# A band mask that is loaded, and one that GpSimd builds: block-sparse attention with a feed-forward layer on one core

## The chip, the cores and the metric

One Trainium2 chip, one core of it. The metric is the device time of one execution in microseconds (us). The kernel before takes 613.03 us, the median of 3 runs (612.43 to 613.39). The engines are TensorE (PE, with its weight loads as PEld), VectorE (DVE), ScalarE (ACT), GpSimd (POOL), and SyncE (SP), whose queue issues every DMA named here.

## The reference

Attention in 4 batches of 8 heads, 768 positions of 64 dimensions. Each query sees the keys at a distance under 16 and, beside them, one summary key and value for each of the 24 blocks of 32 keys: the maximum of the block's keys and the mean of its values.

```python
k_sum = k.reshape(B, H, nb, 32, D).max(axis=3)
v_sum = v.reshape(B, H, nb, 32, D).mean(axis=3)
scores_l = where(|i - j| < 16, scale * q @ k.T, -1e9)
scores_s = scale * q @ k_sum.T + log(32)
a = softmax(concat([scores_l, scores_s]))
x = a @ concat([v, v_sum])
h = x @ w_in;  g = maximum(0.01 * h, h);  out = g @ w_out
```

The result x is 3072 rows of 512; w_in is 512 by 2048, w_out 2048 by 512. All of it is float32.

## The kernel before

The rows are cut into eight chunks of 384 rows (c = 0 to 7, two a batch). Attention of a chunk is 12 units: four pairs of heads (p = 0 to 3) by three tiles of 128 queries. A unit goes through these steps, with the names of its tiles: scores (`s`, PE, line 371), sum with the mask and row minimum of the negated score (`e` and `m`, DVE, line 376), exponential with row sum (`e` and `z`, ACT, line 383), division (DVE, lines 420 to 428), transposition (`t`, PE, line 388), copy (`pt`, ACT, line 439), product with the values (`o`, PE, line 394), and a high part and a low part of x (ACT line 445, DVE line 448). The feed-forward layer of a chunk (PE, `h` line 724, `a` lines 743 to 745) takes each product three times, by high and low parts. The weights come in pieces of 512 KB, and DVE and ACT split each into two parts (lines 680 to 693); the pieces stream in during the first two chunks. Later chunks get their attention beside feed-forward work of earlier ones.

What a pair of heads needs in chunk 0: keys `kn` (410 KB; DVE takes the block maxima, line 248, and copies them into place, line 331, and ACT copies the key windows, line 315), queries `q` (197 KB), value windows `v` (295 KB), and for all pairs together the block means of v. Those are made for batch 0 by six matmuls (`vps`, line 284) from three pieces `vb` (524 KB each) with a matrix of 1/32; ACT copies the result (line 289), and GpSimd copies it behind each pair's value windows (line 327). In the program, `L327` waits for the load of `v` and for the means.

`mask` is one tile of 128 partitions by 404 float32: three versions of the mask of 120 columns (24 for the block scores, which hold sqrt(64) * log 32, and 96 for the window, 0 or -8e9; the first, an inner and the last tile of queries), and behind them 44 columns with the matrix for the block means (called `share` in the change). Line 230 loads it from HBM, where the host had laid it out.

The order of the work is written by a planner in the program (`Plan`, lines 71 to 155). Each operation has a cost, a priority and what it depends on, and the planner replays them: an engine that is free takes the ready operation of lowest priority. The instructions of each engine then stand in that order, and each engine works them off in it. For loads the planner counts 250 bytes a ns, one after the other. `LOADS` fixes the order of the first loads on SP's queue; where one of them must wait (for a buffer), all behind it wait. Two queries' buffers alternate (`KR = 2`), three of values (`VR = 3`), six of `big` for keys, `vb` and weight pieces; the exponentials `e` and the copies `pt` have two buffers of two units each (`ER`, `PTR`).

Where the planner foresees that PE has nothing to do before the feed-forward layer begins, the program puts matmuls on zeros in its queue (`spare`, line 1343), as many as fill the foreseen gap less 300 ns. PE executes them whether or not it could go on earlier.

The constants `PLACE`, `PL`, `VT`, `KP`, `KS`, `XW`, `W0` and `OFF` are offsets of priorities: `OFF` holds those of the steps of a unit in chunks 0 and 1, `VT` that of the block means, `KP` and `KS` those of the key maxima of batch 0, `PL` that of the later steps of pairs of units, `W0` that of the first weight piece. `USQ` is used nowhere.

Of the kernel before, what the change touches and what calls it, by code (L numbers as in the profile page):

```python
# [13 lines left out]
ALU = mybir.AluOpType  # L14
AX = mybir.AxisListType

B, H, S, D = 4, 8, 768, 64
NP = H // 2
BLK, WIN = 32, 16
NS = S // BLK  # L20
# [3 lines left out]
LK = 120  # L24
# [17 lines left out]
P2 = 56.037475  # L42
XB = (0, 1, 1, 0)
SB = 2
PLACE = {0: (0.0, 1.0), 1: (13.07, 0.61), 2: (24.128751, 0.979249), 3: (33.570341, 0.464868), 4: (39.468202, 0.605071), 5: (53.449962, 0.361478), 6: (58.988368, 0.872963), 7: (67.160878, 1.199752)}
PLACE.update({c: (59.84 + UPC * (c - 6), 1.0) for c in range(8, NCH)})
LATE = 23.650498
RS = 8
# [2 lines left out]
AHEAD = 2.529455  # L51
BACC = {"dynamic_dma_scratch_size": 1024}

PL = -1.175
WS = 0.721
WS2 = 0.376
LD = 3.541
XP = 2.116
VT = -1.915
KP = -1.757  # L60
KS = -4
XW = 1
B1 = 2.589473
B2 = 2.761653
USQ = 1.589009
WT = 1.15
W0 = -1.523
WO = 1.029
CUT = 1
WIDE = 12  # L70
OFF = {('rec', 0): (-2.762, -0.036), ('ex', 0): (3.066, -0.083), ('pt', 0): (0.079, -0.747), ('tr', 0): (-2.274, -0.362), ('ttr', 0): (-5.883, 0.424), ('nrm', 0): (0.274, -0.908), ('qk', 0): (-7.35, 0.368), ('xlo', 0): (1.352, 0.149), ('xhi', 0): (-1.785, 0.164), ('av', 0): (-2.699, -0.545), ('pt', 1): (3.776, 0.667), ('xlo', 1): (2.15, -1.485), ('tr', 1): (-0.4, -0.633), ('ttr', 1): (5.204, 0.013), ('qk', 1): (5.855, -0.039), ('av', 1): (-6.304, -0.442), ('ex', 1): (1.869, -0.057), ('nrm', 1): (1.368, -0.059), ('rec', 1): (3.066, -0.235), ('xhi', 1): (-5.461, -0.101)}
LOADS = [('kn', 0, 0), ('q', 0, 1), ('q', 0, 0), ('kn', 0, 1), ('mask',), ('vb', 0, 0), ('kn', 0, 2), ('vb', 0, 2), ('q', 0, 2), ('vb', 0, 1), ('kn', 0, 3), ('w', 0, 0), ('v', 0, 0), ('v', 0, 1), ('q', 0, 3), ('v', 0, 2), ('v', 0, 3), ('w', 1, 0), ('w', 0, 1), ('w', 1, 1)]


class Plan:
# [84 lines left out]
def ACT(n, psum=False, extra=0):  # L160
    return (51 if psum else 93) + 0.833 * n + 93 * extra
# [6 lines left out]
def POOL(n):  # L168
    return 130 + 1.0 * n


def build(tc, ctx, a):
    nc = tc.nc
# [11 lines left out]
    mask = cst.tile([128, 3 * LK + 44], F32, name="mask")  # L185
# [23 lines left out]
    P = Plan()  # L209
# [3 lines left out]
    def load_op(name, prio, fn, **kw):  # L213
        first[name] = P.op("SP", 550, prio, fn, **kw)
        return first[name]

    def new(tag, key, shape, dt=F32, bufs=2, src=None):
        tl[key] = (src or st).tile(shape, dt, tag=tag, name="_".join(str(x) for x in key), bufs=bufs)
        return tl[key]

    def bigs(key):
        n = int(P.slot[key][3:])
        tl[key] = big[:, 1024 * n:1024 * n + 1024]
        return tl[key]
# [2 lines left out]
        tag = tag or P.slot[key]  # L227
        return new(tag, key, [128, 512], src={"h": ps_h, "a": ps_acc, "s": ps_s, "t": ps_t}[tag[0]], bufs=1)

    mask_op = load_op(("mask",), -8.7, lambda: nc.sync.dma_start(out=mask, in_=a["mask"]), size=128 * (3 * LK + 44) * 4)  # L230

    LEAD = UPC + LD
    ksum_op, vsum_op, k_op, v_op, x_op, w_op = {}, {}, {}, {}, {}, {}
# [41 lines left out]
    def v_mean_pe(t):  # L275
        def load(j):
            x = bigs(("vb", 0, j))
            nc.sync.dma_start(out=x.rearrange("p (t d) -> p t d", t=2), in_=a["v0"][j])

        def mm(j, i):  # L280
            if i + j == 0:
                new("a1", ("vps",), [128, 512], src=ps_acc, bufs=1)
            n = 2 * j + i
            nc.tensor.matmul(tl["vps",][:NS], mask[:, 3 * LK + 20 - 4 * n:3 * LK + 44 - 4 * n], tl["vb", 0, j][:, 512 * i:512 * i + 512],  # L284
                             start=n == 0, stop=n == 5)

        def copy():
            tl["vsum", 0] = new("out", ("vs0",), [128, 512], bufs=TPC)[:NS]
            nc.scalar.copy(tl["vsum", 0], tl["vps",][:NS])
        prev = [mask_op]  # L290
        for j in range(3):
            o = load_op(("vb", 0, j), t - 4.5 + 0.1 * j, lambda j=j: load(j), alloc=[("big", ("vb", 0, j), 0)], size=128 * 4096)
            for i in range(2):
                prev = [P.op("PE", 856, t, lambda i=i, j=j: mm(j, i), after=[o] + prev, use=[("vb", 0, j), ("vps",)],
                             alloc=[("a1", ("vps",), 1)] if i + j == 0 else [])]
        vsum_op[0] = P.op("ACT", ACT(512, True), t + 0.1, copy, after=prev, use=[("vps",)], alloc=[("out", ("vsum", 0), TPC)])


    def operands(c, p, t, ahead):
# [12 lines left out]
        def windows(j):  # L312
            k = tl[kk][:, T:].rearrange("p (t r k) -> p t r k", r=2, k=LK)[:, :, j, NS:LK]
            x = tl[kw][:, 64 * j:64 * j + T].rearrange("p (t r) -> p t r", r=128)[:, :, 0:96]
            nc.scalar.copy(k, x)  # L315
# [18 lines left out]
        if cb:  # L334
            kn_op[kw] = load_op(kw, t - 1.3 - ahead, load_k, alloc=[("big", kw, 0)], size=128 * (T + 2 * WIN) * 4)
        ks = [P.op("ACT", ACT(TPC * 96), t - 0.6 + (0 if b else XW), lambda j=j: windows(j), after=[lq, kn_op[kw]], use=[kk, kw]) for j in range(2)]
        lv = load_op(("v", c, p), t - 0.6 - ahead, load_v, alloc=[("v", kv, VR)], size=96 * TPC * 1024)
        if c:
            ls = load_op(("s", c, p), t - 0.3, load_s, after=[lv, vsum_op[b]], use=[kv, ("vsum", b)], size=2 * NS * TPC * 512)
        else:  # L340
            ls = P.op("POOL", POOL(2 * TPC * 128), t - 0.3, load_s, after=[lv, vsum_op[b]], use=[kv, ("vsum", b)])
        ks.append(P.op("DVE", DVE(2 * TPC * NS, True), t - 0.5 + (0 if b else KS), k_s, after=[lq, ksum_op[b, p]], use=[kk, ("ksum", b, p)]))
        k_op[c, p], v_op[c, p] = ks, [lv, ls]

    def place(u, at=None):
        c = min(u // UPC, NCH - 1) if at is None else at
        t, d = PLACE.get(c, (UPC * c, 1.0))
        return t + d * (u - UPC * c)
# [52 lines left out]
    def unit(u):  # L401
        c, r, p, i, mv = where(u)
        K = lambda n: (n, u)
        v, m = place(u), u // 2
        off = lambda n: OFF[n, c][0] + OFF[n, c][1] * r if (n, c) in OFF else 0.0
        kk, kv = ("k", c, p), ("v", c, p)
# [92 lines left out]
    def pair(m):  # L499
# [4 lines left out]
        gs, gt, go = [("g", m + n, ph) for n in range(3)]  # L504
        v1, v2 = v + 2 + PL, v + 4 + PL
        kk, kv = [("k", c, x) for x in sorted({p, p1})], [("v", c, x) for x in sorted({p, p1})]
# [755 lines left out]
    for c in range(NCH):  # L1262
        b, cb = divmod(c, CPB)
        for p in range(NP):
            t = place(TPC * (c * NP + p))
            if cb == 0:
                if b:
                    v_mean(b, p, place(TPC * c * NP) + (B1 if b == 1 else B2) - TPC - 0.5 + 0.6 * p, 0)
                elif p == 0:
                    v_mean_pe(VT)  # L1270
                k_max(b, p, t - TPC - 0.3 + (B1 if b == 1 else B2 if b else KP), 0 if b else 9 - 3 * p)
        for p in range(NP):
            t = place(TPC * (c * NP + p))
            operands(c, p, t, 0 if c else 7 - 2.5 * p)
    for f in range(NF):
        for w in range(2):
            weights(f, w, LEAD - WT + min(f, SPL) * WS + max(f - SPL, 0) * WS2 + WO * w + (W0 if f == 0 else 0))
    for u in range(UPC):
# [42 lines left out]
    for n in range(6):  # L1321
        f = (1, 5, 11)[n % 3]
# [5 lines left out]

    for x, y in zip(LOADS, LOADS[1:]):
        first[y]["behind"] = first[x]  # L1330
# [18 lines left out]
def layouts(q, k, v, moe_w_in, moe_w_out):  # L1349
    import numpy as np  # L1350

    f = np.float32
    qa = q.reshape(B, NP, 2, CPB, T, D).transpose(0, 3, 1, 2, 5, 4).reshape(B, CPB, NP, 128, T)
    kp = np.zeros((B, NP, 128, S + 2 * WIN), f)
    kp[..., WIN:WIN + S] = k.reshape(B, NP, 2, S, D).transpose(0, 1, 2, 4, 3).reshape(B, NP, 128, S)
    vpad = np.zeros((B, NP, S + 2 * WIN, 128), f)
    vpad[:, :, WIN:WIN + S] = v.reshape(B, NP, 2, S, D).transpose(0, 1, 3, 2, 4).reshape(B, NP, S, 128)
    va = np.zeros((B, CPB, NP, 96, 2 * TPC, 128), f)
    for c in range(CPB):
        for i in range(2 * TPC):  # L1360
            o = c * T + 64 * i
            va[:, c, :, :, i] = vpad[:, :, o:o + 96]
    vb = np.ascontiguousarray(v.reshape(B, NP, 2, NS, BLK, D).transpose(0, 1, 3, 2, 5, 4)).reshape(B, NP * NS, 128, BLK)
    v0 = np.ascontiguousarray(v[0].transpose(1, 0, 2).reshape(3, 2, 128, H * D).transpose(0, 2, 1, 3))
    wi = moe_w_in.reshape(4, 128, NF, 128).transpose(2, 1, 0, 3).reshape(NF, 128, 512)
    w = np.ascontiguousarray(np.stack([wi, moe_w_out.reshape(NF, 128, DM)], axis=1)).view(np.int64)
    mk = np.full((128, 3, LK), -8.0e9, f)
    for vnt, t0 in enumerate((0, 128, S - 128)):
        for r in range(128):
            for w_ in range(96):  # L1370
                key = t0 - WIN + w_ + r // 64 * 64
                if 0 <= key < S and abs(t0 + r - key) < WIN:
                    mk[r, vnt, NS + w_] = 0.0
    mk[:, :, 0:NS] = math.sqrt(D) * math.log(BLK)
    mean = np.zeros((128, 44), f)
    mean[np.arange(128), 20 + np.arange(128) // BLK] = 1.0 / BLK
    mk = np.ascontiguousarray(np.concatenate([mk.reshape(128, 3 * LK), mean], axis=1))
    return {"q": np.ascontiguousarray(qa), "k": kp, "v": va, "v0": v0, "vb": vb, "w": w, "mask": mk}


# [16 lines left out]
```

## Time and profile before

| | |
|---|---|
| median of 3 runs | 613.03 us |
| the profiled execution | 612.7 us |
| its span (first to last instruction) | 610.9 us |
| PE busy in the span | 604.9 us (99%) |
| DVE, ACT, POOL busy | 469.7, 351.1, 4.4 us |
| spare matmuls (line 1343) | 164 |
| mean granted PE clock | 1.0 of full speed |
| DMA over the span | 130 MB, 213 GB/s |

The span is 1.8 us shorter than the execution's time. "Busy" of PE holds the spare matmuls too: the real work of PE is less. In the rows below, a line such as L376 is a line of the kernel before; out<-in are names of tiles; PEclk is the granted clock of PE as a share of full speed; a DMA share near 1 means that all 16 DMA engines were at work.

### The profile page before, as it was taken

The numbers are of one execution on the slowest core, as the hardware profiler recorded it, in microseconds if no ns is written. First come the engines' busy times: TensorE is split into PE (matmuls) and PEld (weight loads), VectorE is DVE, ScalarE is ACT, GpSimd is POOL, SyncE is SP. The second block draws the span as 40 slices with busy tenths as digits, with TensorE's granted clock in tenths as the row PEclk, the third lists the DMA queues.
The fourth block names the chain that finished last, engine by engine and source line by source line (L and its number), as shares of the span: only waits on it lengthen the run. The fifth ranks groups of instructions, "written<-read, shape, count | busy, mean of one in ns | idle before, by whom it ended". The sixth has DMA issues, their size and how long they took to land.

```text
span 610.9 us, 12895 instructions
## 1 busy us (share of the span) xinstructions
PE 604.9 (99%) x4676; PEld 540.1 (88%) x4676; DVE 469.7 (77%) x1281; ACT 351.1 (57%) x965; POOL 4.4 (1%) x10
## 2 busy tenths in 40 slices
PE   9999999999999999999999999999999999999997
PEld 6688889889888889999898897989889899999996
DVE  5899999953989995536688875877987783868687
ACT  5899996553776676416466665753717262606060
POOL 0200000000000000000000000000000000000000
PEclk9999999999999999999999999999999999999999
DMA  8898998896878826526497563866757484757552
GB/s 298 245 282 273 288 301 245 269 325 198 288 240 244 252 64 197 167 65 190 120 292 229 175 219 120 280 202 216 257 183 231 143 236 143 237 152 229 156 155 103
DMA packets 82926, 129.99 MB, mean 213 GB/s; under 512 B 7024, under 2 KB 50608, under 8 KB 82864
## 3 DMA queue, kind: packets, MB, share of 16 engines
q1 hardware_dynamic: 82864, 129.18, 68.1%
q8 instruction: 37, 0.61, 0.4%
q14 instruction: 25, 0.20, 0.1%
HBM read 97.72 MB, written 29.36 MB: 208 GB/s over the span
## 4 chain that ended last, share of the span: by engine, by line
PE 91%; DVE 4%; ACT 2%; DMA 1%; issue 0%; SPq 0%; DVEq 0%
PE L L1229 19%; PE h L724 12%; PE X L1090 8%; PE W L1090 8%; PE Z L1090 7%; PE B_a L1040 5%; PE a L744 4%; PE a L745 4%; PE a L743 4%; PE Y L1090 4%; PE B_s L1040 2%; PE B_to L1040 1%; ACT e L383 1%; PE vps L284 1%; DMA big<-in_k_dram 1%; DVE big L687 1%
## 5 line engine op out<-in xcount | busy, mean ns | idle before, releaser
L724 PE MATMUL h<-x,win_hi 128*128 128x384 f32 x320 | 82.7, 339 | 0.0
L383 ACT ACTIVATE e<-e,m 128x120 f32<-128x120 f32 x192 | 73.7, 388 | 3.7 <-DVE m L376 3.5
L1229 PE MATMUL L<-wout_hi,win_hi 128*128 128x512 f32 x168 | 66.5, 396 | 0.0
L1229 PE MATMUL L<-wout_hi,win_lo 128*128 128x512 f32 x168 | 65.7, 391 | 0.0
L1229 PE MATMUL L<-wout_lo,win_hi 128*128 128x512 f32 x168 | 65.6, 391 | 0.0
L724 PEld LDWEIGHTS h<-x,win_hi 128*128 128x128 f32 x320 | 57.6, 188 | 2.3 <-issue 0.2
L724 PE MATMUL h<-x,win_lo 128*128 128x384 f32 x160 | 53.8, 336 | 0.0
L743 PE MATMUL a<-wout_hi,ghi 128*128 128x512 f32 x120 | 48.4, 403 | 0.0
L745 PE MATMUL a<-wout_hi,glo 128*128 128x512 f32 x120 | 47.3, 394 | 0.0
L744 PE MATMUL a<-wout_lo,ghi 128*128 128x512 f32 x120 | 47.1, 392 | 0.1
L1229 PEld LDWEIGHTS L<-wout_hi,win_lo 128*128 128x128 f32 x168 | 31.5, 188 | 6.8
L383 ACT ACTIVATION_READ_ACCUMULATOR e<-e,m 128x1 f32 x192 | 36.7, 191 | 0.0
L1229 PEld LDWEIGHTS L<-wout_lo,win_hi 128*128 128x128 f32 x168 | 31.6, 188 | 5.7
L1229 PEld LDWEIGHTS L<-wout_hi,win_hi 128*128 128x128 f32 x168 | 31.6, 188 | 5.7
L734 DVE TENSOR_TENSOR glo<-gs,ghi 128x384 fp32r<-128x384 f32 x40 | 22.1, 554 | 17.0 <-ACT gs L728 16.3
L731 ACT ACTIVATE ghi<-h 128x384 fp32r<-128x384 f32 x40 | 19.6, 490 | 25.9 <-PE h L724 25.9
L1186 ACT COPY P<-X 128x384 f32<-128x384 f32 x19 | 9.0, 473 | 37.0 <-PE X L1090 36.9
L724 PEld LDWEIGHTS h<-x,win_lo 128*128 128x128 f32 x160 | 30.0, 188 | 0.0
L745 PEld LDWEIGHTS a<-wout_hi,glo 128*128 128x128 f32 x120 | 22.5, 188 | 5.4 <-DVE glo L734 0.4
L315 ACT COPY k<-big 128x288 f32<-128x288 f32 x64 | 24.8, 434 | 4.1 <-DMA big<-in_k_dram 4.0
L744 PEld LDWEIGHTS a<-wout_lo,ghi 128*128 128x128 f32 x120 | 22.6, 188 | 3.9 <-DVE wout_lo L693 0.4
L743 PEld LDWEIGHTS a<-wout_hi,ghi 128*128 128x128 f32 x120 | 22.6, 188 | 3.3
(620 smaller groups left out, 1625.9 us busy)
## 6 DMA issues: line engine op xcount, KB each, us to landing
win_hi<-sums SPq DMA_DIRECT2D x73, 256.0 KB
win_lo<-sums SPq DMA_DIRECT2D x71, 256.0 KB
big<-in_w_dram SPq DMA_DIRECT2D x32, 512.0 KB
sums<-big SPq DMA_DIRECT2D x32, 512.0 KB
v<-in_v_dram SPq DMA_DIRECT2D x32, 288.0 KB
big<-in_k_dram SPq DMA_DIRECT2D x16, 400.0 KB
k<-in_q_dram SPq DMA_DIRECT2D x32, 192.0 KB
wout_hi<-sums SPq DMA_DIRECT2D x21, 256.0 KB
```

The source lines that it names most:

```text
L315: nc.scalar.copy(k, x)
L383: nc.scalar.activation(out=e[:, n], in_=e[:, n], func=AF.Exp, scale=-1.0, bias=m[:, n:n + 1], accum_out=z[:, n:n + 1])
L724: nc.tensor.matmul(h[:, :T], w[:, 512 * f + 128 * k:512 * f + 128 * k + 128], x[:, T * k:T * k + T], start=n == 0, stop=n == 11)
L731: nc.scalar.activation(out=gnew(tag, G("ghi", f)), in_=tl[G("h", f)][:, :T], func=AF.Prelu, alpha=0.01)
L734: nc.vector.tensor_tensor(out=gnew(tag, G("glo", f)), in0=tl[G("gs", f)], in1=tl[G("ghi", f)].bitcast(F32), op=ALU.subtract)
L743: nc.tensor.matmul(o, gh, wout_hi[:, f], start=f == f0, stop=False)
L744: nc.tensor.matmul(o, gh, wout_lo[:, f], start=False, stop=False)
L745: nc.tensor.matmul(o, gl, wout_hi[:, f], start=False, stop=f == f1 - 1)
L1040: nc.tensor.matmul(o[:, x:x + 256], g, w[l], start=fresh and m == 0, stop=m == 5, skip_group_check=True)
L1090: nc.tensor.matmul(o[:, :T], w[:, l, 128 * k:128 * k + 128], x[y][:, T * k:T * k + T], start=start and n == 0, stop=n == 5, skip_group_che ...
L1186: nc.scalar.copy(tmp(K("P1")), ps("X"))
L1229: nc.tensor.matmul(o, g, w[:, f], start=s + m == 0, stop=s == 1 and m == 5)
```

## The change

Nothing is loaded for `mask` any more, and the host no longer lays it out. GpSimd builds the tile in eleven steps: a memset of the 3 x 96 window columns and one of the 3 x 24 block columns, two selections for each half of the partitions, which write -8e9 outside the band, two small memsets for the keys ahead of the first and behind the last; and for `share` a memset and two selections. The first eight make the mask, which the sums of line 376 wait for; the first `vps` matmul waits for all eleven. They stand in GpSimd's queue right behind the identity matrix that it makes already.

The list `LOADS` is in a new order, without the mask, and 11 constants and most entries of `OFF` for chunk 0, with some for chunk 1, have new values.

```diff
-LOADS = [('kn', 0, 0), ('q', 0, 1), ('q', 0, 0), ('kn', 0, 1), ('mask',), ('vb', 0, 0), ('kn', 0, 2), ('vb', 0, 2), ('q', 0, 2), ('vb', 0, 1), ('kn', 0, 3), ('w', 0, 0), ('v', 0, 0), ('v', 0, 1), ('q', 0, 3), ('v', 0, 2), ('v', 0, 3), ('w', 1, 0), ('w', 0, 1), ('w', 1, 1)]
+LOADS = [('q', 0, 0), ('kn', 0, 0), ('kn', 0, 1), ('vb', 0, 2), ('vb', 0, 0), ('q', 0, 1), ('q', 0, 2), ('vb', 0, 1), ('kn', 0, 3), ('kn', 0, 2), ('w', 0, 0), ('v', 0, 0), ('v', 0, 1), ('q', 0, 3), ('v', 0, 2), ('v', 0, 3), ('w', 1, 0), ('w', 0, 1), ('w', 1, 1)]
...
-PL = -1.175
+PL = -1.839248
...
-VT = -1.915
-KP = -1.757
-KS = -4
-XW = 1
+VT = -1.498859
+KP = -1.697158
+KS = -5.644761
+XW = 1.171242
...
-W0 = -1.523
+W0 = -1.126317
...
-    mask_op = load_op(("mask",), -8.7, lambda: nc.sync.dma_start(out=mask, in_=a["mask"]), size=128 * (3 * LK + 44) * 4)
+    bands = mask[:, :3 * LK].rearrange("p (v k) -> p v k", k=LK)
+    share = mask[:, 3 * LK:]
+    LOW = -8.0e9
+
+    def select(x, fill, base, step, up):
+        n = [[step, y] for y in x.shape[1:]] if len(x.shape) == 2 else [[0, x.shape[1]], [step, x.shape[2]]]
+        return lambda: nc.gpsimd.affine_select(out=x, in_=x, compare_op=ALU.is_ge, fill=fill, base=base, pattern=n, channel_multiplier=up)
+
+    fill = lambda x, y: lambda: nc.gpsimd.memset(x, y)
+    steps = [(288, fill(bands[:, :, NS:], 0.0)), (72, fill(bands[:, :, :NS], math.sqrt(D) * math.log(BLK)))]
+    for r in range(2):
+        x = bands[64 * r:64 * r + 64, :, NS:]
+        steps += [(288, select(x, LOW, -1, 1, -1)), (288, select(x, LOW, 31, -1, 1))]
+    steps += [(16, fill(bands[:64, 0, NS:NS + 16], LOW)), (16, fill(bands[64:, 2, NS + 80:], LOW))]
+    steps += [(44, fill(share, 1.0 / BLK)), (44, select(share, 0.0, 20 * BLK, -BLK, 1)), (44, select(share, 0.0, -20 * BLK + BLK - 1, BLK, -1))]
+    mask_op = share_op = None
+    for n, (size, fn) in enumerate(steps):
+        share_op = P.op("POOL", POOL(size), -30 + 0.01 * n, fn, after=[share_op] if n else [])
+        mask_op = share_op if n < 8 else mask_op
...
-        prev = [mask_op]
+        prev = [share_op]
```

## Rows read from the trace of the kernel before

**Rows 1.** Busy time of the engines in nine stretches of the span (us from its start): the stretch, its length, then busy us and number of instructions of each engine, the granted clock, the DMA share and the rate.

```profile
core 0: us, PE busy (x) PEld busy (x) DVE busy (x) ACT busy (x) POOL busy (x), PEclk, DMA share, GB/s
0.00:5.94 5.94, 4.95 (x65) 4.85 (x69) 1.30 (x3) 2.05 (x3) 0.70 (x6) 1.00 0.70 224
5.94:12.60 6.66, 6.38 (x79) 3.46 (x80) 5.40 (x31) 4.28 (x19) 0.00 (x0) 1.00 0.96 350
12.60:21.56 8.96, 8.93 (x88) 4.68 (x86) 6.44 (x34) 6.69 (x24) 0.98 (x2) 1.00 1.02 279
21.56:29.76 8.20, 8.17 (x137) 5.96 (x136) 6.70 (x38) 7.66 (x35) 2.68 (x3) 1.00 0.71 225
29.76:34.00 4.24, 4.24 (x60) 3.53 (x59) 3.79 (x13) 4.06 (x11) 0.00 (x0) 1.00 1.04 286
34.00:100.00 66.00, 65.92 (x482) 57.33 (x480) 64.41 (x175) 60.44 (x153) 0.00 (x0) 1.00 0.93 283
```

**Rows 2.** The same stretches for line 1343 alone, the spare matmuls (here the columns are PE and PEld only).

```profile
0.00:5.94 5.94, 4.95 (x61) 4.77 (x61) 1.00 0.70 224
5.94:12.60 6.66, 1.41 (x23) 1.33 (x24) 1.00 0.96 350
12.60:21.56 8.96, 3.27 (x48) 2.83 (x47) 1.00 1.02 279
21.56:29.76 8.20, 1.64 (x21) 1.15 (x19) 1.00 0.71 225
29.76:34.00 4.24, 0.79 (x14) 0.78 (x14) 1.00 1.04 286
```

**Rows 3.** Timeline of the first 9 us, all engines: start, length, engine, line, operation; in brackets how long the engine had been idle and what ended that.

```profile
0.73 0.20 POOL masks.py:197 MEMSET ident<- 128x128 f32 x1 [0.29 <-POOLq L1387]
0.74 0.39 SPq L244 DMA_DIRECT2D big<-in_k_dram  x1
1.01 0.29 POOL masks.py:199 TENSOR_SCALAR_AFFINE_SELECT ident<-ident 128x128 f32<-128x128 f32 x1
...
2.60 0.43 SPq L230 DMA_DIRECT2D mask<-in_mask_dram  x1
...
3.90 0.95 DVE L248 TENSOR_REDUCE ksum<-big 128x24 f32<-128x768 f32 x1 [2.97 <-DMA big<-in_k_dram]
...
4.89 0.23 DVE L331 COPY k<-ksum 128x144 f32<-128x144 f32 x1
5.86 0.64 PE L371 MATMUL s<-k 64*64 64x120 f32 x16
...
6.81 0.95 DVE L248 TENSOR_REDUCE ksum<-big 128x24 f32<-128x768 f32 x1 [1.69 <-DMA big<-in_k_dram]
7.68 0.27 DVE L376 CUSTOM_DVE_ANT_0 e<-s,mask 128x120 f32<-128x120 f32 x1
8.87 0.33 SPq L310 DMA_DIRECT2D k<-in_q_dram  x1
```

**Rows 4.** The chain of waits that ended last, from 14 to 54.6 us: start, length, what the chain ran through.

```profile
18.08 1.83 PE vps L284 x4
19.91 1.73 PE spare L1343 x29
21.63 0.61 PE o L394 x16
22.25 0.44 PE spare L1343 x6
22.70 0.45 PE o L394 x8
23.16 0.38 PE t L388 x2
23.53 0.02 issue
23.56 0.28 DVE e L376
...
53.85 0.68 DVE wout_lo L693
54.57 0.50 PE a L744
```

**Rows 5.** Timeline from 14 to 32 us: the copies that the first product with v waits for, and a subtraction of DVE that ran beside one of them.

```profile
19.94 0.57 ACT L289 COPY vs<-vps 24x512 f32<-24x512 f32 x1 [1.51 <-PE vps L284]
20.58 3.66 POOL L327 COPY v<-vs 24x768 f32<-24x768 f32 x4 [19.28 <-ACT vs L289]
21.11 0.83 DVE L693 TENSOR_TENSOR win_lo<-big,win_hi 128x512 fp32r<-128x512 f32 x1 [0.74 <-ACT win_hi L690]
```

**Rows 6.** That subtraction in general, and the copies of line 327 (least, middle and greatest length in ns, first and last start).

```profile
L693 DVE TENSOR_TENSOR win_lo<-big,win_hi x6: 683/684/830, 21.1 to 53.2; 128x512 fp32r<-128x512 f32 x6
L327 POOL COPY v<-vs x4: 815/854/1284, 20.6 to 23.4; 24x768 f32<-24x768 f32 x4
```

**Rows 7.** Groups of ACT's instructions from 5.94 to 34 us: busy us and mean ns of one, idle time before them.

```profile
L383 ACT ACTIVATE e<-e,m 128x120 f32<-128x120 f32 x24 | 9.2, 387 | 0.5 <-DVE m L376 0.4
L315 ACT COPY k<-big 128x288 f32<-128x288 f32 x8 | 3.2, 434 | 2.1 <-DMA big<-in_k_dram 2.1
```

More of the change, by code (lines that the diff above doesn't have):

```diff
@@ L44 @@
 SB = 2
-PLACE = {0: (0.0, 1.0), 1: (13.07, 0.61), 2: (24.128751, 0.979249), 3: (33.570341, 0.464868), 4: (39.468202, 0.605071), 5: (53.449962, 0.361478), 6: (58.988368, 0.872963), 7: (67.160878, 1.199752)}
+PLACE = {0: (0.0, 1.0), 1: (13.07, 0.61), 2: (24.006994, 0.984093), 3: (33.570341, 0.464868), 4: (39.468202, 0.605071), 5: (53.449962, 0.361478), 6: (58.988368, 0.872963), 7: (67.160878, 1.199752)}
 PLACE.update({c: (59.84 + UPC * (c - 6), 1.0) for c in range(8, NCH)})
@@ L58 @@
 XP = 2.116
-VT = -1.915
-KP = -1.757
-KS = -4
-XW = 1
+VT = -1.498859
+KP = -1.697158
+KS = -5.644761
+XW = 1.171242
 B1 = 2.589473
 B2 = 2.761653
-USQ = 1.589009
+USQ = 0.996052
 WT = 1.15
-W0 = -1.523
+W0 = -1.126317
 WO = 1.029
@@ L70 @@
 WIDE = 12
-OFF = {('rec', 0): (-2.762, -0.036), ('ex', 0): (3.066, -0.083), ('pt', 0): (0.079, -0.747), ('tr', 0): (-2.274, -0.362), ('ttr', 0): (-5.883, 0.424), ('nrm', 0): (0.274, -0.908), ('qk', 0): (-7.35, 0.368), ('xlo', 0): (1.352, 0.149), ('xhi', 0): (-1.785, 0.164), ('av', 0): (-2.699, -0.545), ('pt', 1): (3.776, 0.667), ('xlo', 1): (2.15, -1.485), ('tr', 1): (-0.4, -0.633), ('ttr', 1): (5.204, 0.013), ('qk', 1): (5.855, -0.039), ('av', 1): (-6.304, -0.442), ('ex', 1): (1.869, -0.057), ('nrm', 1): (1.368, -0.059), ('rec', 1): (3.066, -0.235), ('xhi', 1): (-5.461, -0.101)}
-LOADS = [('kn', 0, 0), ('q', 0, 1), ('q', 0, 0), ('kn', 0, 1), ('mask',), ('vb', 0, 0), ('kn', 0, 2), ('vb', 0, 2), ('q', 0, 2), ('vb', 0, 1), ('kn', 0, 3), ('w', 0, 0), ('v', 0, 0), ('v', 0, 1), ('q', 0, 3), ('v', 0, 2), ('v', 0, 3), ('w', 1, 0), ('w', 0, 1), ('w', 1, 1)]
+OFF = {('rec', 0): (-3.490984, -0.036), ('ex', 0): (2.417329, -0.083), ('pt', 0): (0.046959, -0.898369), ('tr', 0): (-0.749481, -0.362), ('ttr', 0): (-4.901411, 0.280477), ('nrm', 0): (4.374486, -0.945439), ('qk', 0): (-4.074091, 0.087513), ('xlo', 0): (1.444887, 0.149), ('xhi', 0): (-2.921188, 0.151739), ('av', 0): (-3.09307, -0.292385), ('pt', 1): (3.008952, 0.667), ('xlo', 1): (2.15, -1.194642), ('tr', 1): (-0.4, -0.633), ('ttr', 1): (5.204, 0.013), ('qk', 1): (5.855, -0.187375), ('av', 1): (-6.304, -0.633333), ('ex', 1): (1.869, -0.282207), ('nrm', 1): (1.368, -0.059), ('rec', 1): (3.066, -0.235), ('xhi', 1): (-5.461, -0.101)}
+LOADS = [('q', 0, 0), ('kn', 0, 0), ('kn', 0, 1), ('vb', 0, 2), ('vb', 0, 0), ('q', 0, 1), ('q', 0, 2), ('vb', 0, 1), ('kn', 0, 3), ('kn', 0, 2), ('w', 0, 0), ('v', 0, 0), ('v', 0, 1), ('q', 0, 3), ('v', 0, 2), ('v', 0, 3), ('w', 1, 0), ('w', 0, 1), ('w', 1, 1)]
 class Plan:
@@ L1366, in layouts @@
     w = np.ascontiguousarray(np.stack([wi, moe_w_out.reshape(NF, 128, DM)], axis=1)).view(np.int64)
[L1367 to L1378, printed above, removed]
+    return {"q": np.ascontiguousarray(qa), "k": kp, "v": va, "v0": v0, "vb": vb, "w": w}
 def kernel(**inputs):
```

## The prediction

> **What bounds the kernel now.** I read first the busy time by stretches [rows 1], then the spare matmuls in the same stretches [rows 2], then the chain of waits over the beginning [rows 4], and last the timeline of the first 9 us [rows 3].
>
> From 34 us on PE is busy for 65.92 of 66 us [rows 1], with next to no spares left. What is gained must come from the first 34 us, and it must reach the end by starting the full stretch earlier. After 5.94 us and before 34 us spares take 1.41 + 3.27 + 1.64 + 0.79 = 7.11 us of PE [rows 2]; that is the most a new start could free.
>
> Who sets that start? The chain runs through PE's own queue up to 23.5 us: the block means (`vps`) to 19.91, then 29 spares for 1.73 us, then the first product with v at 21.63. From 23.56 to 54.57 it runs through DVE and ACT, and ends in a product of PE [rows 4]. DVE and ACT are almost full there: ACT idles 8.20 - 7.66 = 0.54 us from 21.56 to 29.76 and 0.18 us from 29.76 to 34, and DVE 1.59 us from 34 to 100 [rows 1]. So a gain survives only if the whole of the beginning moves forward, PE's, ACT's and DVE's work together. A spare removed from PE alone would come back as a wait at about 54 us.
>
> Ahead of that stands the DMA. From 5.94 to 21.56 us its share is 0.96 and 1.02 [rows 1]: loads come as fast as they can, and the beginning goes as the bytes come.
>
> **The mask's load goes.** It is 128 x 404 x 4 = 206,848 bytes. All loads behind it move forward by its time: 0.59 us at the 350 GB/s of the stretch to 12.60, 0.74 us at the 279 GB/s of the one to 21.56 [rows 1]. The front of the chain moves alike, for another reason: the first sum with the mask (7.68) does not wait for the mask but stands behind the second block maximum of DVE, which started at 6.81 when the second piece of keys had landed [rows 3]. Ahead of and with that piece there were 410 + 197 + 197 + 410 = 1,213 KB, and now there are 197 + 410 + 410 = 1,017 KB. The 197 KB at 350 GB/s are 0.56 us: 6.81 becomes 6.25, the first sum comes at about 7.1. At the other end, the first value windows have 4,829 KB up to their end and will have 4,622 KB, again the mask's bytes. Both ends agree, so the first product with v should move by 0.6 to 0.75 us; I take 0.7. That PE follows is likely because the planner counts loads by bytes: with fewer ahead of the value windows it foresees a smaller gap and puts fewer spares. SP's issue of the mask (0.43 us [rows 3]) goes too, worth nothing: the queue stands still after the next loads until 8.87, waiting for a buffer of q.
>
> **GpSimd builds the tile.** The trace has a selection of 128 columns at 0.29 us and a memset of 128 at 0.20 us [rows 3]. A selection of 288 columns costs between 0.29 us (all fixed) and 0.66 us (all by column); I take the upper end, since only that could hurt. Four are 2.64 us, the large memset 0.45 us, three small ones under 0.2 us each, 3.7 us for eight steps; with 0.08 us between steps, as between the two of the identity matrix (0.93 to 1.01), 4.3 us. They start at 1.30 behind the identity, so the mask is there between 3.5 and 5.7 us, against a first use at 7.1. The three steps of `share` end by 6.8 us at the most (0.29 each), needed when the first `vps` runs; its piece of v lands later than that. GpSimd has nothing else to do until 20.58 [rows 5], so nothing queues behind. Price: nothing, covered by the wait for keys; without that cover each us that the mask is late would be one of the chain.
>
> A cost could still come through contention. A subtraction of DVE took 0.83 us beside a GpSimd copy, where the middle one takes 0.684, and the longest GpSimd copy 1.284 against 0.854 [rows 5, 6]: the two engines do slow each other, by 0.15 and 0.43 us. The only DVE work with something at stake during the build is the copy of block maxima (0.23 us [rows 3]) at about 5.5 us; a delay of 0.66 us puts the first scores at 6.4 us, and they still lie ahead of the first sum.
> The Trainium skill, "SBUF — State Buffer", section "Who interferes with whom", says more sharply that the port which the two share is locked for a whole instruction, that a VectorE copy can take it, and that the later one stands still until the first ends. By that rule the build could end at 5.9 us rather than 5.7, which the 1.2 us that are left still cover; it lifts the chance of a late mask, below, from 3 to 5 in 100.
>
> **The new order of loads.** q of the second pair falls from second to sixth place: with it 2,262 KB. By the rates of [rows 1] 1,331 KB are there at 5.94 us and the rest needs 931 / 350 = 2.7 us, so 8.6 us; the second keys landed some 1.4 us after their bytes by the same reckoning (1,213 / 224 = 5.4 against 6.8), so q lands at about 10 us. The first three units give ACT 6 x 0.387 = 2.3 us of exponentials [rows 7], to about 9.8 us. The next are then at most a few tenths late, and two buffers of `e` hold up everything past the eighth unit until the first product with v anyway. Price: nothing.
>
> The last piece of v for the block means has 2,983 KB up to its end instead of 3,600: 617 / 350 = 1.8 us earlier. This takes the means off the path: today 1.72 us (ACT 0.57, GpSimd 0.95 or so) lie between the last `vps` and the first product [rows 4, 5].
>
> The keys of the third pair fall from seventh to tenth place: 3,803 KB, there at about 13.1 us by the rates, landed at 14.5, then a block maximum (0.95) and a copy (0.23): third scores at 15.7 at the earliest. I cost it at nothing, since ACT is idle for 8.96 - 6.69 = 2.27 us from 12.60 to 21.56 [rows 1]; the third rival is what happens if that cover fails.
>
> **The priorities.** They can take spares after the first product with v, 1.64 + 0.79 us [rows 2], but ACT's idle time of 0.54 + 0.18 = 0.72 us there is the bound above. Below, they could lose as much by a worse order. The value is nearest to that idle time; I take somewhat under half of it, 0.3 us, as a gain, because the steps of the first pairs reach this stretch earlier than the bytes alone make them (their means of v are done 1.8 us sooner), so that more is ready where PE now fills up.
>
> **Sum.** 0.7 + 0.3 = 1.0 us. From the profiled execution, 612.7 (span 610.9 and 1.8 around it), 611.7. The median stands 0.33 above that execution, so 612.0 is what I forecast.
>
> **Rivals.**
> First, more than the bytes: the means are early, so the 1.73 us of spares before the first product [rows 4] go as well, if the planner had put them there for the means and not for the value windows. For it: GpSimd's first copy, 20.58 to about 21.5, ends just before the product. Against it: the value windows stand behind the same keys and the first weight piece as before, only the mask fewer. Time: 613.0 - 0.7 - 1.7 = 610.6.
>
> Second, the transfer is hidden: the spares in PE's queue (3.27 us before 21.56) mean that PE arrives by its own queue and not by the bytes. For it: the value windows should have landed some us before 21.6. If the new plan has as many spares, nothing is gained: 613.0.
>
> Third, slower: work that ACT did early is late. With the third scores go two window copies and the exponentials of units 7 and 8, 2 x 0.434 + 4 x 0.387 = 2.4 us [rows 7]. If they come after the first product, they meet an ACT with 0.54 us idle: 2.4 - 0.5 - 0.7 of earlier start = 1.2 us slower, 614.2. It decides when the third scores start after 20.8 - 2.4 = 18.4 us. For it: these scores ran at 14.65 in PE's order until now, and spares may be put ahead of them. Against it: the 2.27 us of idle ACT.
>
> Fourth, the change doesn't do what it says: the mask is late, because a selection on GpSimd takes over twice its upper bound; four at 1.3 us would put it at about 8.4, 1.3 us behind the first sum's place: 613.3 after the gain of 1.0.
>
> **How the numbers follow.** Forecast 0.40, first rival 0.20, second 0.18, third 0.17, fourth 0.05. The likeliest one's own range is 611.3 to 612.7 (transfer 0.6 to 0.75, priorities -0.4 to 0.7, and 0.3 of scatter). The range reaches to 610.4 for most of the first rival and 614.2 for the third. I call 0.2% (1.2 us, about what a measurement of this kernel can tell from no change) the bound: faster is under 611.8, slower over 614.25. Faster: 0.40 x 0.4 + the first rival's 0.20 = 0.36, with 0.02 for luck among the rest 0.38. Slower: half of the third and of the fourth, 0.11, and 0.05 for a later stall that I can't see (DVE has 1.59 us of room from 34 to 100 us). Within: 0.46.
>
> **What would show it.** First sum with the mask at about 7.1 us; GpSimd's last mask step before 6 us; q of the third pair issued at about 8.3 instead of 8.87; first product with v at about 20.9; the first full run of feed-forward products, which ended the last spares at 33.97 or so, about 1 us earlier; and from there PE as full as before. Wrong if the first sum waits for GpSimd, if the third scores start after 18.4, or if PE waits near 54 us for DVE by as much as the start was earlier.

## The result, and the profile after

The changed kernel takes 617.41 us (median of 4 runs, 616.51 to 618.11) against 613.21 for the kernel before beside it: a ratio of 1.0069, 95% interval 1.0057 to 1.0082. It is slower by 4.2 us. The forecast was 612.0, the range 610.4 to 614.2. The span of the profiled execution grew from 610.9 to 616.2 us. The mean granted clock was 0.999 or 1.000 in all four executions, so the 4.2 us are not a matter of the clock.

The same stretches as in [rows 1], of the changed kernel:

```profile
0.00:5.94 5.94, 4.88 (x54) 4.85 (x54) 1.24 (x3) 2.05 (x3) 3.56 (x17) 1.00 0.60 173
5.94:12.60 6.66, 5.33 (x70) 3.41 (x67) 4.11 (x24) 3.42 (x15) 0.00 (x0) 1.00 0.70 246
12.60:21.56 8.96, 8.90 (x80) 3.63 (x79) 6.16 (x28) 5.59 (x21) 1.22 (x2) 1.00 0.97 312
21.56:29.76 8.20, 7.38 (x127) 5.11 (x124) 7.34 (x44) 7.67 (x34) 2.56 (x3) 1.00 0.74 217
29.76:34.00 4.24, 3.99 (x49) 3.40 (x49) 3.74 (x17) 3.63 (x15) 0.00 (x0) 1.00 1.01 300
34.00:100.00 66.00, 64.70 (x510) 55.81 (x507) 62.14 (x172) 59.25 (x152) 0.00 (x0) 1.00 0.89 272
```

And its spares (here line 1361) in four of them, as in [rows 2]:

```profile
5.94:12.60 6.66, 2.55 (x40) 2.07 (x37) 1.00 0.70 246
12.60:21.56 8.96, 1.57 (x19) 1.15 (x19) 1.00 0.97 312
21.56:29.76 8.20, 1.13 (x14) 0.79 (x14) 1.00 0.74 217
...
34.00:100.00 66.00, 2.07 (x31) 1.82 (x31) 1.00 0.89 272
```

How to read them: PE loses time as idle time (length less busy) and as spares. From 5.94 to 34 us that was 0.34 + 7.11 = 7.45 us before, and is 2.46 + 6.08 = 8.54 now (0.83 us of spares lie in the stretch left out). From 34 to 100 us it was 0.08 + 0.16 = 0.24 and is 1.30 + 2.07 = 3.37. So 1.1 us are lost ahead of 34 us and 3.1 behind it, 4.2 of the 5.3 us by which the span grew. And DVE and ACT have done less work by 21.56 us: DVE 1.24 + 4.11 + 6.16 = 11.51 against 13.14, ACT 11.06 against 13.02.

The timeline of the changed kernel, lines that answer to [rows 3]:

```profile
1.66 1.93 POOL L236 TENSOR_SCALAR_AFFINE_SELECT mask<-mask 64x288 f32<-64x288 f32 x4
...
4.17 0.51 POOL L236 TENSOR_SCALAR_AFFINE_SELECT mask<-mask 128x44 f32<-128x44 f32 x2
4.78 0.95 DVE L266 TENSOR_REDUCE ksum<-big 128x24 f32<-128x768 f32 x1 [3.77 <-DMA big<-in_k_dram]
...
7.49 0.95 DVE L266 TENSOR_REDUCE ksum<-big 128x24 f32<-128x768 f32 x1 [1.49 <-DMA big<-in_k_dram]
8.36 0.27 DVE L394 CUSTOM_DVE_ANT_0 e<-s,mask 128x120 f32<-128x120 f32 x1
...
19.87 0.64 PE L389 MATMUL s<-k 64*64 64x120 f32 x16
...
22.32 0.69 PE L412 MATMUL o<-pt,v 120*64 120x64 f32 x16
```

GpSimd has finished all eleven steps at 4.68 us, long before the first sum with the mask. That sum stands, as before, behind the second block maximum of DVE, but the keys for it landed at 7.47 instead of 6.79. The third scores run at 19.87 instead of 14.65, the first product with v at 22.32 instead of 21.56. The chain of waits then shows how late the full stretch of feed-forward products begins: at 37.16 us, behind the last spares. Before, the timeline has it at 33.97:

```profile
33.97 0.63 PE L724 MATMUL h<-x,win_hi 128*128 128x384 f32 x2
```

In the changed kernel's chain:

```profile
35.88 1.28 PE spare L1361 x21
37.16 2.68 PE h L742 x15
```

And the list of what PE waited for from 60 to 100 us has a wait at 84 us that was not there:

```profile
PE s_('g', 13, 1)_1335 L412 <- DVE x L557: 1.1, 1, 1.1
PE to_('g', 12, 1)_1292 L406 <- DVE e L540: 0.2, 1, 0.2
```

### The profile page after: what moved, and what is told of

It is laid out like the page before. It is cut to its first block, busy times and chain, and to the rows that moved or that the text cites. A ratio compares the mean times of both kernels' runs of the same rounds, so it can differ in the third digit from the quotient of the medians.

```text
span 616.2 us, 12921 instructions
## 1 busy us (share of the span) xinstructions
PE 606.5 (98%) x4679; PEld 540.5 (88%) x4679; DVE 470.1 (76%) x1281; ACT 351.0 (57%) x965; POOL 7.3 (1%) x21
## 4 chain that ended last, share of the span: by engine, by line
PE 92%; DVE 4%; DMA 1%; ACT 1%; issue 1%; SPq 0%; DVEq 0%
PE L L1247 19%; PE h L742 13%; PE W L1108 8%; PE X L1108 7%; PE Z L1108 7%; PE B_a L1058 5%; PE a L761 4%; PE a L763 4%; PE a L762 4%; PE Y L1108 4%; PE B_s L1058 2%; PE B_to L1058 1%; DMA big<-in_k_dram 1%; PE vps L302 1%; PE t L406 1%
```

## The experiments

**First, the parts of the change apart.** Each of the four kernels is the changed one with a part taken back.

```diff
 # e1: old LOADS without ('mask',), all old constants
 # e2: old LOADS without ('mask',), new constants
 # e3: new LOADS, all old constants
 # e4: the change, with one entry moved
-... ('q', 0, 1), ('q', 0, 2), ('vb', 0, 1), ('kn', 0, 3), ('kn', 0, 2), ('w', 0, 0) ...
+... ('q', 0, 1), ('vb', 0, 1), ('kn', 0, 3), ('kn', 0, 2), ('q', 0, 2), ('w', 0, 0) ...
```

> The mask built by GpSimd, with the old order of loads (the mask's own entry left out) and all old constants. Theory A (the order of loads: q of the third pair in seventh place stops SP's queue when only 2,262 KB are on their way, the DMA engines run dry from 8.5 to 12.5 us): 612.3 to 613.0, the DMA share from 8 to 12.5 us near 1. Rival B (GpSimd's build itself slows the first loads: 173 GB/s instead of 224 in the first 5.94 us): 614 or more, the first 5.94 us again near 175 GB/s. Rival C (the new constants make a worse order later on, up to the wait of PE near 84 us): 612.3 to 613.0 as with A.

> The change with the old order of loads (without the mask's entry), new constants kept. A: 612.5 to 614. B: as the changed kernel or 1 us under it. C: 616 to 618, with the wait of PE near 84 us.

> The mask built by GpSimd, the new order of loads, all old constants. A: 616 to 618, DMA share from 8.5 to 12.5 us near 0.5 as in the changed kernel. B: as the changed kernel or a little under it. C: 612.5 to 613.5.

> The change with one entry of the order moved: q of the third pair goes behind the keys of the third pair, so that 1,344 KB more are on their way before SP's queue stops. A: 614 to 615.5, since about 2 us of idle DMA engines go (sum of the missing shares from 8 to 12.5 us); the share there near 1. B and C: 617, as the changed kernel.

Measured, with the kernel before at 613.41: e1 620.15 (1.0101, 1.0084 to 1.0118), e2 622.86 (1.0152, 1.0137 to 1.0167), e3 620.99 (1.0123, 1.0105 to 1.0141), e4 620.20 (1.0104, 1.0085 to 1.0123). All are slower than the changed kernel, and no theory holds in all four. (B's time of 614 or more came true in e1, but the rate in its first 5.94 us was 213 GB/s, not near 175.) The mask alone (e1), which should have been nearly free, costs 6.7 us; the new order of loads and the new constants together win back a part of that. Neither of the two has a price of its own: the new constants cost 2.7 us with the old order of loads (e2 against e1) and win 3.6 us with the new one (the changed kernel against e3). What all four share, beside GpSimd's build, is that the planner no longer counts the mask's load and so writes other orders. That became theory D.

**Second, the same orders with another mask.** Here the planner still counts a load of the mask, so that the queues of PE, DVE, ACT and SP stand instruction by instruction as in the kernel before; only the function behind that entry differs. e7 lets SP issue the first loads in the new order, and e6 moves one load in SP's queue of the changed kernel, each without a new plan.

```diff
 # e5
-    mask_op = load_op(("mask",), -8.7, lambda: nc.sync.dma_start(out=mask, in_=a["mask"]), size=128 * (3 * LK + 44) * 4)
...
+    def build_mask():
+        for size, fn in steps:
+            fn()
+
+    mask_op = load_op(("mask",), -8.7, build_mask, size=128 * (3 * LK + 44) * 4)
 # e7: e5, and behind P.order()
...
+    spots = sorted(todo.index(first[x]) for x in want)
+    for n, x in zip(spots, want):
+        todo[n] = first[x]
 # e6: the change, and behind P.order()
+    held = first["q", 0, 2]
+    todo.remove(held)
+    todo.insert(todo.index(first["kn", 0, 2]) + 1, held)
```

> The kernel before with every queue of instructions as it stood on PE, DVE, ACT and SP (the spares too), only the mask's load left out and its eleven steps on GpSimd instead; the planner still counts the load. Theory D (the time follows the orders that the planner writes, and these were in step with the chip only for the plan of before; the mask's source matters little): 612.0 to 613.5, first sum with the mask at 7.1 to 7.7 us. Rival B (GpSimd's build delays the first loads or engines): 615 or more, with 213 GB/s or less in the first 5.94 us.

> As the kernel with the orders kept and the mask on GpSimd, but SP issues the first loads in the new order, q of the third pair in seventh place; PE, DVE, ACT as before. Theory A: 614.5 or more, DMA share from 8.5 to 12.5 us about 0.5. Theory D alone: under 614.

> The changed kernel with the orders of PE, DVE, ACT and GpSimd as they are, only SP issues q of the third pair behind the keys of the third pair. Theory A (the loads run dry from 8.5 to 12.5 us behind that q): 615.0 to 616.3, the idle time of PE from 5.94 to 12.6 us (1.33 us) and from 21.56 to 29.76 (0.82 us) mostly gone. Theory D alone: within 0.7 us of 617.4.

> The kernel before, unchanged, for a second profile. If the time at which the spares get faster (30 of 61 at 107 ns each in the first profile, the others at 56) belongs to the kernel: again 4.95 us for the 61. If it changes from execution to execution: another time, up to 6.4 us (61 at 105 ns), with a time of 612.4 to 614.6 all the same.

Measured, with before at 613.54: e5 613.64 (1.0003, 0.9994 to 1.0013), e7 618.98 (1.0099, 1.0073 to 1.0124), e6 617.95 (1.0074, 1.0057 to 1.0091), e8 612.73 (one run).

e5 says that the build and the missing transfer together are worth nothing when all orders and spares are kept. (It lies 0.1 us above D's range, and its first sum with the mask came at 7.92 where D said 7.1 to 7.7.) The time alone doesn't exclude that a cost of the one hides a gain of the other; but in e5's trace GpSimd has ended all eleven steps at 4.68 us, no sum waits for them, and the first 5.94 us have 221 GB/s against 224 before. No cost of the build shows, so rival B falls. e5 and e1 do the same work with the same loads and constants and differ by 6.5 us, in nothing but the order in which the engines' instructions stand and the spares among them: with the load uncounted the planner writes 192 spares instead of 164. e6 fills the stretch in which the DMA engines ran dry (5.94 to 12.60 us has 246 GB/s in the changed kernel and 378 in e6) and gains nothing, so theory A falls; and e5 has two dry microseconds of its own, at 9 to 11 us, at no cost.

e7 expected under 614 by theory D alone and 614.5 or more by A, and took 619. Two things are mixed in it. Loads that come in another order than the one that PE's queue was written for leave PE idle, and then the granted clock falls (the third number from the right in these lines of e7):

```profile
12.60:21.56 8.96, 6.62 (x45) 3.35 (x45) 3.42 (x20) 2.67 (x10) 0.00 (x0) 0.69 0.99 307
21.56:29.76 8.20, 8.20 (x58) 3.03 (x56) 4.79 (x23) 4.70 (x18) 0.37 (x1) 0.75 0.31 81
```

All four executions of e7 had a mean granted clock of 0.991 to 0.996; no other kernel of this group went below 0.998. So e7 shows that an order of loads which the other queues don't match can be dear; how much of it is waiting and how much the clock, it doesn't show. That e7 is no proof of A rests on e6.

**Third, where in the plan the loss lies.** A prefix of one plan, and everything else in the order of another plan, is again an order that keeps all dependencies. e9 and e10 splice the plan of e5 (load counted) and that of e1 (not counted) where the planner's clock is at 40 us. e11 and e12 disturb the planner in the kernel before itself; the mask is loaded there.

```diff
 # e9 (e10: plan(False), plan(True))
+    one, two = plan(True), plan(False)
+    head = [(o, t) for o, t in one if t < 40000]
...
+    for o, t in head + [(o, t) for o, t in two if id(o) not in done_ids]:
+        o["at"] = t
+        todo.append(o)
 # e11: what the planner counts, not what is loaded
-    size=128 * (3 * LK + 44) * 4)
+    size=1)
 # e12
-    LAT = {"SP": 910.0, ...
+    LAT = {"SP": 960.0, ...
```

> A splice of two plans with the same loads, mask on GpSimd and old constants: what the planner places in its first 40 us comes from the plan that counts the mask's load (613.64 us as a whole), everything after it in the order of the plan that does not count it (620.15 as a whole). D1 (the order of the beginning decides, and what is late later is late because of it): 613 to 614.5. D2 (the later order is worse by itself: PE waits of 0.86 us from 60 to 100 us and of 3.5 us from 100 to 300 us in the uncounted plan): 617 to 619.

> The reverse splice: the first 40 us of the plan that does not count the load, then the order of the plan that does. D1: 618 to 620. D2: 614 to 616, with no wait of PE over 1 us from 60 to 300 us.

> The kernel before with its mask loaded as before, but the planner counts that load as one byte; the chip moves the same bytes. Theory D (orders in step with the chip for one plan only): 616 to 622. If the order of the planner mattered little and the removal itself cost the time: 612.5 to 614.

> The kernel before with one number of the planner changed that has nothing to do with the mask: it adds 960 ns instead of 910 to each load. All work, loads and priorities are as before. Theory D: 614.5 to 620, for any small shift in the plan puts other orders. Otherwise: 612.5 to 614.

Measured, with before at 613.31: e9 622.54 (1.0137, 1.0107 to 1.0166), e10 614.39 (1.0010, 1.0000 to 1.0020), e11 616.42 (1.0048, 1.0034 to 1.0061), e12 614.33 (1.0018, 1.0007 to 1.0029).

D2 holds in direction: the start of the uncounted plan is worth about 1 us (e10, in D2's range), the order behind it the rest and more. e9 lies 4 us above D2's 617 to 619, and above e1 too; a splice is an order that no plan was replayed for, which may have a cost of its own. What PE waited for from 60 to 300 us in e9:

```profile
PE s_('A', 13)_2951 L391 <- DVE x L634: 2.2, 1, 2.2
PE to_('B', 12)_2913 L408 <- ACT y L782: 0.9, 1, 0.9
PE s_('B', 12)_2912 L414 <- DVE m L396: 0.8, 1, 0.8
PE s_('g', 13, 1)_1333 L414 <- DVE x L559: 0.7, 1, 0.7
PE h L744 <- DVE win_lo L713: 0.2, 1, 0.2
```

In e10 the same list is empty. The waits are mostly for single instructions in the queues of DVE (`x`, `m`) and ACT (`y`); the list doesn't say what ahead of them could have stood elsewhere. The longest ended at 222.5 us, some 180 us behind the splice. Behind it the clock falls: from 224 to 226 us PE is busy throughout, at a granted clock of 0.51, close to the lower level of 1.2 GHz:

```profile
224.00:226.00 2.00, 2.00 (x9) 2.00 (x8) 1.97 (x11) 1.37 (x3) 0.00 (x0) 0.51 0.80 244
```

So a part of the loss of e9 and e1 is the clock: the one execution of e9 with a mean granted clock of 1.000 took 619.55 us, the three at 0.993 to 0.996 622.16 to 623.40; of e1 the one at 1.000 took 618.97, the three at 0.996 or 0.997 619.92 to 621.26. At full clock, in that one execution, e1 still lost 5.6 us.

e11 shows that the planner's count is enough: the chip moves the same bytes, and 3 us are lost. e12 is a milder result: another number changed, 1 us lost, under what I had put down for D; a disturbance does not always cost much.

**Fourth, spares and waits.** Can the loss be had back by taking out what PE is seen to lose? e13 and e16 leave out the spares behind the first scores, e14 lets DVE do the part that PE waits for at 84 us ahead of two others; e15 is e5 unchanged, for a second profile (its label misnames it).

```diff
 # e13 (the change), e16 (e5)
-begun = o.get("mlp", False)
...
 until = o["at"] + o["cost"]
+begun = True
 # e14
+moved = x_op[1][9]
+for o in [o for o in todo[:todo.index(moved)] if o["eng"] == "DVE"][:-3:-1]:
+    todo.remove(o)
+    todo.insert(todo.index(moved) + 1, o)
```

> The changed kernel with all orders as they are, but without the spare matmuls behind the first scores (113 of 167 go). E (the start is late because PE works through gaps that the planner foresaw, 2.07 us of spares from 34 to 60 us among them): 614.5 to 616.5. F (what PE would do next is not ready either, for ACT and DVE work in an order that puts it late; spares only fill that time): 617 to 618, the removed spares turning into idle time of PE.

> The changed kernel with two instructions of DVE's queue (parts of a weight piece's split) put behind the low part of x that PE waits for at 84 us, which was ready at 82.74 and ran at 83.78; nothing else moves. If that wait is a loss of its own (1.07 us of PE): 616.2 to 616.8. If DVE's lateness there comes back at the next instruction: 617.2 or more.

> The kernel with the orders of before and the mask on GpSimd once more, unchanged, for a second profile: it was 613.64. In the first profile its first spares took 6.04 us against 4.95 and 5.08 in the two profiles of before. If GpSimd's build makes the spares slower: 5.9 us or more again; if it is chance: any value from 4.9 to 6.4.

> The same orders as before with the mask on GpSimd, and no spares behind the first scores (103 of 164 go). E: 610.5 to 612.5, faster than both kernels, since PE goes on as soon as its data are there. F: 613 to 614.5.

Measured, with before at 613.17: e13 624.40 (1.0176, 1.0157 to 1.0194), e14 617.87 (1.0070, 1.0054 to 1.0087), e15 612.98 (one run), e16 617.56 (1.0056, 1.0029 to 1.0083, single runs from 612.67 to 620.27).

Leaving the spares out makes both kernels slower, the changed one by 7.0 us (against its 617.41), the one with the orders of before by 4.4. Neither E nor F said that. The stretches of e13 (the third number from the right is the granted clock):

```profile
5.94:12.60 6.66, 3.43 (x37) 1.55 (x34) 4.04 (x23) 3.38 (x15) 0.00 (x0) 0.74 0.77 274
12.60:21.56 8.96, 8.88 (x43) 2.36 (x42) 4.62 (x24) 4.09 (x18) 0.00 (x0) 0.81 1.01 275
21.56:29.76 8.20, 5.89 (x77) 3.67 (x76) 6.21 (x29) 6.52 (x24) 3.64 (x4) 0.78 0.45 114
29.76:34.00 4.24, 4.24 (x50) 2.89 (x48) 2.79 (x20) 2.54 (x11) 0.00 (x0) 0.50 0.99 344
34.00:60.00 26.00, 24.02 (x183) 20.37 (x183) 21.45 (x73) 21.18 (x64) 0.00 (x0) 0.82 0.88 252
```

PE now idles where the spares were (3.23 us of the first stretch, 2.31 of the third), and the clock falls: to 0.50 throughout 29.76 to 34 us, which is 1.2 of 2.4 GHz, though PE is busy all of that stretch. With the spares it was 1.00 in each. So here the spares keep the clock up, and this run can't tell E from F. e16 can, for its own orders, because its ten executions differ in the clock: three with a mean granted clock of 1.000 took 612.67, 613.09 and 613.44 us, seven at 0.986 to 0.992 took 616.33 to 620.27. Where the clock held, leaving out 103 spares changed the time by a few tenths at most (the kernel before took 613.17 beside it). That is close to F's 613 to 614.5: the late spares only fill time there, and what they buy is the clock.

e14 lost the wait at 84 us and won nothing. From 60 to 100 us PE waited in it for

```profile
PE a L762 <- DVE wout_lo L711: 0.6, 1, 0.6
PE a L761 <- DVE out L778: 0.2, 1, 0.2
```

The number is the one I gave for "comes back at the next instruction", but the trace doesn't show that. The wait of 0.6 us lies between 60 and 65 us, ahead of the two instructions that were put back (84.16 us and later), so they did not cause it. PE reached the products in front of the wait at 82.02 us, 1.17 later than in the changed kernel (80.85), and DVE's `x` ran at 83.82 in the one and 83.78 in the other: the wait is gone in this profile because PE came late. What moving `x` is worth, e14 doesn't show.

**Last, the changed kernel's own plan, spliced.** The planner runs twice in one program, once with the priorities, `LOADS` and counted mask of before, once with those of the change (360 priorities differ); the splice is as in e9. The mask is built by GpSimd in both.

> Splice for the changed kernel itself: what the planner places in the first 40 us is the plan of before (its order of loads and constants; mask on GpSimd), everything later in the order of the changed kernel's plan. S (the changed kernel loses in its beginning: DVE and ACT have done 1.6 and 2.0 us less work by 21.56 us than before, and never make it up): 613 to 614.7. R (the later order loses, as it did in the plan with the old constants): 616 to 622.

> The reverse splice: the first 40 us as the changed kernel plans them (its order of loads and constants), everything later in the order of before. S: 616 to 618.5. R: 613.5 to 615.

Measured, with before at 613.36: e17 616.32 (1.0056, 1.0044 to 1.0069), e18 615.26 (1.0036, 1.0022 to 1.0049). e17 lies in R's range and e18 between R's and S's, so both hold in part. The new start with the old order behind it costs 1.9 us; the old start with the new order behind it 3.0 us; the whole change 4.2 beside its own runs of before. The two add up to a little more than the whole. The mean granted clock was 0.998 to 1.000 in all ten executions, so these are losses by waiting and by spares.

From 34 to 100 us, e17 first and then e18:

```profile
34.00:60.00 26.00, 24.19 (x194) 20.16 (x192) 23.30 (x77) 22.82 (x65) 0.00 (x0) 1.00 0.88 260
60.00:100.00 40.00, 38.71 (x273) 33.37 (x273) 38.42 (x94) 35.41 (x85) 0.00 (x0) 1.00 0.92 276
```

```profile
34.00:60.00 26.00, 25.95 (x235) 22.74 (x236) 24.85 (x82) 24.67 (x72) 0.00 (x0) 1.00 0.91 281
60.00:100.00 40.00, 40.00 (x285) 35.23 (x284) 39.56 (x95) 35.71 (x84) 0.00 (x0) 1.00 0.95 284
```

e17 starts as the kernel before does (PE busy for 12.41 of 12.44 us from 21.56 to 34 us in both) and then idles for 1.81 and 1.29 us, with DVE and ACT less busy. What its PE waited for:

```profile
PE h L744 <- DVE win_lo L713: 1.3, 2, 1.0
...
PE s_('g', 13, 1)_1332 L414 <- DVE x L559: 0.9, 1, 0.9
PE a L764 <- DVE wout_lo L713: 0.6, 1, 0.6
```

e18 has the changed kernel's deficit of DVE and ACT at 21.56 us and its spares from 34 to 60 us, and from 60 to 300 us not one wait.

## Why the prediction was wrong

**Right: GpSimd's price.** The eight steps of the mask ended at 3.91 us, inside the 3.5 to 5.7 I gave; a selection of 288 columns took 0.436 us, between the bounds of 0.29 and 0.66. No run shows a cost, and the fourth rival (a late mask) did not come.

**Wrong: the mask's load, 0.7 us.** e5 leaves it out with all orders kept, and the ratio is 1.0003, with an upper end of gain at 0.06%, 0.4 us. The second rival, the transfer hidden at 613.0, is what this part alone does. The busy DMA engines misled me: from 5.94 to 21.56 us they were full, and yet the orders, with the spares in them, set the pace. The step from the load to PE failed as well: I let the planner, with fewer bytes to count, put fewer spares, but with the load uncounted and nothing else changed it put 192 instead of 164 (e1). Nor do loads land as my reckoning by bytes had it. The second keys had 1,017 KB up to their end instead of 1,213 and landed 5.75 us after their issue (1.72 to 7.47) instead of 4.67 (2.12 to 6.79); the first sum came at 8.36 where I put 7.1. Why they were slower isn't shown.

**Wrong: the start, with the order of loads at nothing and the priorities at a gain.** The changed kernel's own start costs 1.9 us with the later order of before behind it (e18). About 1 us is what the uncounted load alone does to a start (e10, with the old order of loads and the old constants); the rest isn't split between the order of loads and the priorities. The mark that I gave for the third rival came true: the third scores started after 18.4 us, at 19.87, and ACT was 1.96 us behind by 21.56. Its direction was right and its 1.2 us near 1.9, in part by luck, since about half of the 1.9 comes with the uncounted load. That the late third scores are the cause is not shown: in e2 they ran at 15.32 and that kernel was slower still.

**Wrong: "and from there PE as full as before".** This is the step that cost most, and no rival held it. I priced the load, its order and the priorities one by one, each by what it does in the first 34 us, and took the order behind that as given. But the planner replays the whole program: one load less in its count, or a priority moved, and the instructions of all four engines stand differently up to 200 us on. In the stretch where DVE has 1.59 us of room in 66, some of these orders leave PE waiting. For the changed kernel that is 3.0 us (e17). It can't be put down to the priorities: the uncounted load writes a worse later order without them (e1 against e5, e9 against e10, and e11), and on the new order of loads the new constants make the kernel faster, not slower. The few per cent that I left "for a later stall that I can't see" were the main case.

**Half shown: the coupling of DVE and PE.** I wrote that a gain of PE alone would come back as a wait near 54 us. The three executions of e16 at full clock fit that: 103 spares fewer in PE's queue, and no gain. Where the time came back no trace shows, for the profiled execution of e16 was one in which the clock fell. e14, which was to show such a trade at 84 us, doesn't.

One sum of the prediction was also wrong: by its own terms (a gain of 0.6 for the transfer, a loss of 0.4 for the priorities) the likeliest case's own range reaches to 612.8, and 613.1 with the scatter, not to 612.7. The measured 617.41 lies outside either way.

Still open: what in the changed plan makes the later order worse, and why the orders of before are good. e12, a small disturbance, costs 1 us and e1 6.7; the runs don't tell what makes the difference. No version here beats the kernel before; e5 equals it with one load and one input less.

## What to carry to other kernels

Where a planner in the program writes the queues of all engines, an edit has two effects: what it does to the chip, and what it does to the plan. Measure them apart, by keeping the orders and swapping the work (e5), and by keeping the work and splicing the orders (e9, e10, e17, e18); an edit that is free by the first may cost 1% by the second. Read the granted clock of every execution beside such a comparison, since an order that leaves PE idle can lose a second time by the clock (e7, e9, e16). A busy share near 1, of DMA engines or PE, does not by itself say that less of that work ends sooner: ask whose queue is waited for.

## What the runs showed of the hardware

The spares' effect on the clock is large, and it isn't certain: without the late ones three of ten executions of e16 kept a mean granted clock of 1.000, and seven lost 3 to 7 us with it at 0.986 to 0.992. In the changed kernel without them the granted clock was 0.50 in a stretch in which PE never idled (e13, 29.76 to 34 us), after stretches in which it was busy for 3.43 of 6.66 us and 5.89 of 8.20.

The first 61 spares took 4.95 and 5.08 us in the two profiles of before, 6.04 and 5.68 in the two of e5, and 6.40 in e1, where all of them come 105 ns apart; in the first profile 30 come at 107 ns and the others at 56. The column of the granted clock has 1.00 for these stretches all the same. The moment at which they get faster differs between executions. GpSimd's build is not needed for a late one, nor does it always bring one: where the mask is loaded too, the first 61 took 5.63 us (e11), and where it is built, 4.91 (e17). e5 lost nothing by it.

A subtraction of DVE can take longer beside GpSimd than [rows 5, 6] showed. In the changed kernel one of the split's subtractions ran beside a GpSimd copy for its first 0.72 us (the copies end at 23.16), and took 1.27 us instead of the usual 0.68; it stands on the chain of waits. In [rows 5] one that ran wholly beside such copies took 0.83, so the size isn't explained.

```profile
20.34 2.82 POOL L345 COPY v<-vs 24x768 f32<-24x768 f32 x3 [15.66 <-ACT vs L307]
22.44 1.27 DVE L711 TENSOR_TENSOR win_lo<-big,win_hi 128x512 fp32r<-128x512 f32 x1
```

The Trainium skill, "SBUF — State Buffer", section "Who interferes with whom", says that a VectorE instruction with two inputs in SBUF contends with a GpSimd instruction that reads SBUF; these lines agree with it. The copy of block maxima, for which I had weighed that page, ran at 5.76 us, behind the end of the build at 4.68, so no run here tests it there.
